# Rounding of the dense weights moved from ScalarE to transfers issued by GpSimd, and pooling of the first group's values by TensorE products

## The chip, the cores and the metric

One core of a Trainium2 chip runs the whole program. The metric is the device time of one execution in microseconds (us). The kernel before takes 1383.42 us, the median of three executions (1382.21 to 1384.28).

## The reference

Three layers on 4608 tokens (batch 8, sequence 576, 8 heads of 64, so d_model is 512):

```python
# attention with keys and values averaged over 8 neighbours in the sequence
k_p = k.reshape(B, H, Sp, 8, D).mean(axis=3)        # Sp = 72
v_p = v.reshape(B, H, Sp, 8, D).mean(axis=3)
attn = softmax(q @ k_p.T / sqrt(64)); x = attn @ v_p
# dense layer, 512 -> 2048 -> 512
h = x @ w_in
x = (maximum(h, 0) + log1p(exp(-abs(h)))) @ w_out
# eight experts, one for each token whose skip score is positive, 512 -> 1024 -> 512
out = x + gate * (maximum(x @ w1[e], 0) @ w2[e])
```

Inputs and outputs are float32. The program multiplies in the type fp32r after splitting each operand into a rounded part and the remainder (`wh` and `wl` for weights, `xh` and `xl` for tokens, `gh` and `gl` for the activation), with three products for each pair.

## The kernel before, in words

The tokens go through attention and the dense layer in nine groups of 512 (`for g in range(NG)`). For a group, `units_of` makes four units, one for each pair of heads: `unit0` for the first group, `unit` for the others. A unit is a Python generator; each `yield` hands over to the next piece of work, and `feed.tick()` advances all of them. The dense layer of a group has 16 chunks of 128 hidden columns. `p1(g, c)` makes twelve 128x512 products (L710), then softplus by three ScalarE activations (L713 to L715), a VectorE maximum-and-add (L716), the rounding of the result on ScalarE (L718) and its remainder on VectorE (L720). `p2(g, c)`, two chunks later, adds twelve products (L731 to L733) into four output banks. After the nine groups comes the expert layer.

The dense weights are loaded once, during the first group. They lie in memory as packed words, and `load_weights` unpacks them in steps that are interleaved with the first group's chunks: `unpack` is two ScalarE activations, `join` two VectorE operations. Chunks 0 to 3 take the path in halves of 512 columns (`half`). Chunks 4 to 15 are handled as six pairs `i` = 2 to 7: two 1 MB transfers (L506), then for each chunk of the pair `unpack` and `join` on 128x1024 into a scratch tile `v`; then for each chunk the rounded part by ScalarE (L519) and the remainder by VectorE (L520). The rounded and remainder parts land in the slot that held the packed words.

The values' pooling in `unit0`: `sums` adds groups of eight neighbours on VectorE (L553), `values` transposes the 72 sums with a TensorE transpose (L560) and copies the result out on ScalarE (L562). The attention weights are transposed by TensorE too (L607), after GpSimd has multiplied them (L546), and `output` makes the products L569.

Up to the expert layer a scheduler places the instructions: it sets the order of each engine's queue from the program and its own costs, so a line that moves in the program also moves lines around it. Each engine runs its queue strictly in order. Most plain transfers are issued by SP (SyncE); GpSimd's queue (POOL) holds the indirect transfers of the later stages and, in the first group, only the memset L643 and the multiplication L546 of each unit. The slots `w0` to `w7` of `wpool` hold one pair's weights each; during the first group's attention slots 5 to 7 serve as the room of `boot2`, `boot_kv` and `boot`.

Of the kernel before, what the change touches and what calls it, by code (L numbers as in the profile page):

```python
# [9 lines left out]
F32 = mybir.dt.float32  # L10
F32R = mybir.dt.float32r
BF16 = mybir.dt.bfloat16
I32 = mybir.dt.int32
U32 = mybir.dt.uint32
AF = mybir.ActivationFunctionType
# [5 lines left out]
P = 128  # L21
# [4 lines left out]
SP = 72  # L26
# [9 lines left out]
def tile_kernel(ctx, tc, qT, kT, vT, wbits, w9, w1, w2, out):  # L36
    nc = tc.nc
# [379 lines left out]
    def wtile(slot, name, *shape, dtype=F32):  # L417
        return wpool.tile([P, *shape], dtype, tag=f"w{slot}", name=name)

    with ExitStack() as ph:  # L420
# [29 lines left out]
        def room(tag, n, first):  # L450
            if first:
                taken[tag] += 1
                return boots[tag][(taken[tag] - 1) % len(boots[tag])][:, :n]
            pool = qp if tag in ("q", "st") else ep
            return pool.tile([P, n], F32, tag=tag, name=tag)
# [7 lines left out]
        def load_weights():  # L463


            bits = wbits.bitcast(I32)

            def unpack(lo, hi):
                nc.scalar.activation(out=hi.bitcast(F32), in_=hi.bitcast(F32), func=AF.Copy,
                                     scale=2.0 ** -112)  # L470
                nc.scalar.activation(out=lo, in_=lo.bitcast(U32), func=AF.Copy, scale=7.49 * 2.0 ** -32)

            def join(v, lo, hi):
                nc.vector.scalar_tensor_tensor(out=v, in0=hi, scalar=3, in1=lo,
                                               op0=ALU.logical_shift_left, op1=ALU.bitwise_or)
                nc.vector.scalar_tensor_tensor(out=v, in0=hi, scalar=-0x80000000, in1=v,
                                               op0=ALU.bitwise_and, op1=ALU.bitwise_or)

            def half(c, j, first):
                wh, wl = (wt[c // 2][:, c % 2, i, j * 512:(j + 1) * 512] for i in range(2))  # L480
                if first:
                    raw = room("raw", 1024, True).bitcast(I32).rearrange("p (a b) -> p a b", b=2)
                else:
                    raw = scratch.tile([P, 512, 2], I32, tag="raw", name="raw")
                nc.sync.dma_start(out=raw.rearrange("p a b -> p (a b)"),
                                  in_=bits[c * P:(c + 1) * P, j * 1024:(j + 1) * 1024])
                lo, hi = raw[:, :, 0], raw[:, :, 1]
                unpack(lo, hi)
                yield
                join(lo, lo, hi)  # L490
                nc.scalar.activation(out=wh, in_=lo.bitcast(F32), func=AF.Copy)
                yield
                nc.vector.tensor_tensor(out=wl, in0=lo.bitcast(F32), in1=wh.bitcast(F32),
                                        op=ALU.subtract)
                yield

            for i in range(EARLY // 2):
                wt.append(wtile(i, f"wt{i}", 2, 2, 1024, dtype=F32R))
            for c in range(EARLY):
                for j in range(2 if c >= LAG else 1):  # L500
                    yield from half(c, j, True)
            for i in range(EARLY // 2, 8):
                raw = wtile(i, f"raw{i}", 2, 1024, 2, dtype=I32)
                for j in range(2):
                    c = 2 * i + j
                    nc.sync.dma_start(out=raw[:, j].rearrange("p a b -> p (a b)"), in_=bits[c * P:(c + 1) * P, :])  # L506
                vs = []
                for j in range(2):
                    lo, hi = raw[:, j, :, 0], raw[:, j, :, 1]
                    unpack(lo, hi)  # L510
                    yield
                    v = scratch.tile([P, 1024], I32, tag="raw", name="v")
                    join(v, lo, hi)
                    vs.append(v.bitcast(F32))
                    yield
                wt.append(wtile(i, f"wt{i}", 2, 2, 1024, dtype=F32R))
                for j in range(2):
                    wh, wl = wt[i][:, j, 0], wt[i][:, j, 1]
                    nc.scalar.activation(out=wh, in_=vs[j], func=AF.Copy)  # L519
                    nc.vector.tensor_tensor(out=wl, in0=vs[j], in1=wh.bitcast(F32), op=ALU.subtract)  # L520
                    yield
            for c in range(LAG):
                yield from half(c, 1, False)
# [25 lines left out]
        def sums(us, vr):  # L549
            for u, *_ in us:  # L550
                kp, v, vp = pooled[u]
                if vp is None:
                    nc.vector.tensor_reduce(vr, v.rearrange("p (s w) -> p s w", w=8), AX.X, ALU.add)  # L553
# [21 lines left out]
        def unit0(hp, us, xh, xl):  # L575
# [20 lines left out]
            shares(e, sm, rc)  # L596
            yield
            yield
            vr = room("vr", SP, True)
            sums(us, vr)  # L600
            yield
            values(us, vr, ps_h, "h")
            et = room("et", 2 * G, True).rearrange("p (a k) -> p a k", a=2)[:SP]
            for h in range(2):
                tr = ps_a.tile([P, 512], F32, tag="pa", name="tr")
# [400 lines left out]
```

## Time and profile before

| | |
|---|---|
| median of three executions | 1383.42 us |
| the profiled execution, its own time | 1373.79 us |
| its span on the core | 1372.1 us |
| TensorE busy (PE) | 1333.0 us, 97% of the span |
| VectorE busy (DVE) | 850.9 us, 62% |
| ScalarE busy (ACT) | 595.4 us, 43% |
| GpSimd busy (POOL) | 312.6 us, 23% |
| mean granted TensorE clock | 0.992 |

The profile is one execution; its own time lies 9.6 us under the median, and its span 1.7 us under its own time. A share of busy time is a mean over very different stages: attention of the first group (0 to 37 us), the first group's dense layer with the loading of weights (37 to about 150 us), the other eight groups, and the experts. A row of the trace names an engine, a line, the operation and `out<-in`; PEld is TensorE's weight load, which runs beside PE.

### The profile page before, as it was taken

The numbers are of one execution on the slowest core, as the hardware profiler recorded it, in microseconds if no ns is written. First come the engines' busy times: TensorE is split into PE (matmuls) and PEld (weight loads), VectorE is DVE, ScalarE is ACT, GpSimd is POOL, SyncE is SP. The second block draws the span as 40 slices with busy tenths as digits, with TensorE's granted clock in tenths as the row PEclk, the third lists the DMA queues.
The fourth block names the chain that finished last, engine by engine and source line by source line (L and its number), as shares of the span: only waits on it lengthen the run. The fifth ranks groups of instructions, "written<-read, shape, count | busy, mean of one in ns | idle before, by whom it ended". The sixth has DMA issues, their size and how long they took to land. (4 is left out here: it accounts for less than half of the span.)

```text
span 1372.1 us, 21243 instructions
## 1 busy us (share of the span) xinstructions
PE 1333.0 (97%) x6970; PEld 1107.9 (81%) x6970; DVE 850.9 (62%) x1955; ACT 595.4 (43%) x1076; POOL 312.6 (23%) x374
## 2 busy tenths in 40 slices
PE   5989999999999999999999999999999999999986
PEld 3767877877877878878778778889999898989986
DVE  7997694784884974974955946555554432326254
ACT  6986544554544545455545445551111111114142
POOL 2000012021121121121030120243333343424343
PEclk9899999999999999999999999999999999999998
DMA  7643343142241241341430311503323222325272
GB/s 272 234 144 80 93 127 97 53 116 68 66 127 44 76 128 31 89 114 43 110 83 8 97 48 39 193 16 111 97 69 98 70 63 73 84 61 173 66 261 91
DMA packets 149599, 134.16 MB, mean 98 GB/s; under 512 B 100789, under 2 KB 116789, under 8 KB 146912
## 3 DMA queue, kind: packets, MB, share of 16 engines
q1 hardware_dynamic: 131744, 95.51, 24.1%
q0 software_dynamic: 17728, 37.13, 8.5%
q8 instruction: 59, 0.97, 0.3%
q14 instruction: 68, 0.56, 0.1%
HBM read 166.67 MB, written 29.67 MB: 143 GB/s over the span
## 5 line engine op out<-in xcount | busy, mean ns | idle before, releaser
L710 PE MATMUL h<-xh,wt 128*128 128x512 f32 x1152 | 381.6, 392 | 3.8 <-DVE a L716 3.8
L710 PEld LDWEIGHTS h<-xh,wt 128*128 128x128 f32 x1152 | 217.2, 189 | 52.3 <-DVE a L716 5.6
L731 PE MATMUL y<-wt,gh 128*128 128x512 f32 x576 | 232.7, 404 | 0.0
L889 PE MATMUL h<-xt,w1h 128*128 128x256 f32 x1280 | 227.9, 282 | 3.9 <-ACT w1h L404 2.1
L119 DVE CUSTOM_DVE_ANT_0 junk<-rows,w9b 128x512 bf16<-128x512 f32 x324 | 222.9, 688 | 8.1 <-ACT rows L113 3.2
L732 PE MATMUL y<-wt,gh 128*128 128x512 f32 x576 | 225.6, 392 | 0.0
L710 PE MATMUL h<-xl,wt 128*128 128x512 f32 x576 | 225.3, 391 | 0.0
L733 PE MATMUL y<-wt,gl 128*128 128x512 f32 x576 | 224.5, 390 | 0.3 <-DVE gl L720 0.3
L889 PEld LDWEIGHTS h<-xt,w1h 128*128 128x128 f32 x1280 | 197.5, 189 | 6.3 <-ACT w1h L404 2.5
L889 PE MATMUL h<-xt,w1l 128*128 128x256 f32 x640 | 180.3, 282 | 1.4 <-DVE w1l L405 0.8
L893 ACT ACTIVATE hs<-h 128x512 fp32r<-128x512 f32 x80 | 47.7, 598 | 298.7 <-PE h L889 222.3
L718 ACT ACTIVATE gh<-a 128x512 fp32r<-128x512 f32 x144 | 90.8, 631 | 167.8 <-DVE a L716 167.7
L716 DVE SCALAR_TENSOR_TENSOR a<-h,a 128x512 f32<-128x512 f32 x144 | 98.7, 685 | 100.2 <-ACT a L715 99.5
L713 ACT ACTIVATE a<-h 128x512 f32<-128x512 f32 x144 | 85.7, 595 | 172.2 <-PE h L710 171.6
L731 PEld LDWEIGHTS y<-wt,gh 128*128 128x128 f32 x576 | 108.1, 188 | 34.3 <-ACT a L713 7.4
L733 PEld LDWEIGHTS y<-wt,gl 128*128 128x128 f32 x576 | 108.1, 188 | 23.9 <-DVE gl L720 0.7
L710 PEld LDWEIGHTS h<-xl,wt 128*128 128x128 f32 x576 | 108.7, 189 | 22.8 <-issue 0.7
L732 PEld LDWEIGHTS y<-wt,gh 128*128 128x128 f32 x576 | 108.3, 188 | 20.7 <-issue 0.8
L889 PEld LDWEIGHTS h<-xt,w1l 128*128 128x128 f32 x640 | 122.8, 192 | 1.8 <-DVE w1l L405 1.0
L720 DVE TENSOR_TENSOR gl<-a,gh 128x512 fp32r<-128x512 f32 x144 | 99.3, 690 | 39.9 <-ACT gh L718 39.5
L917 DVE SCALAR_TENSOR_TENSOR ys<-y,xg 128x512 f32<-128x512 f32 x38 | 28.5, 751 | 147.3 <-PE y L915 147.3
L915 PE MATMUL y<-w2h,hs 128*128 128x512 f32 x304 | 118.4, 389 | 0.0
(196 smaller groups left out, 1817.3 us busy)
## 6 DMA issues: line engine op xcount, KB each, us to landing
w9b<-w SPq DMA_DIRECT2D x81, 256.0 KB
raw<-wbits SPq DMA_DIRECT2D x12, 1024.0 KB
x2d<-rows SPq DMA_DIRECT2D x36, 260.0 KB
et<-q SPq DMA_DIRECT2D x256, 32.0 KB
kv<-kT SPq DMA_DIRECT2D x28, 288.0 KB
kv<-vT SPq DMA_DIRECT2D x28, 288.0 KB
xm<-misc SPq DMA_DIRECT2D x160, 32.0 KB
misc<-misc SPq DMA_DIRECT2D x144, 32.0 KB
```

What stands on the lines that cost most here:

```text
L119: nc.vector.tensor_tensor_reduce(out=ws["junk"], in0=rows[t][:, :D], in1=w9b[e], scale=1.0, scalar=0.0, op0=ALU.mult, op1=ALU.add, accum_o ...
L710: nc.tensor.matmul(h, lhsT=l, rhs=r[:, kk, :], start=n == 0, stop=n == 11)
L713: nc.scalar.activation(out=a, in_=h, func=AF.Abs)
L716: nc.vector.scalar_tensor_tensor(out=a, in0=h, scalar=0.0, in1=a, op0=ALU.max, op1=ALU.add)
L718: nc.scalar.activation(out=gh, in_=a, func=AF.Copy)
L720: nc.vector.tensor_tensor(out=gl, in0=a, in1=gh.bitcast(F32), op=ALU.subtract)
L731: nc.tensor.matmul(y, lhsT=th, rhs=wh, start=c == 0, stop=False)
L732: nc.tensor.matmul(y, lhsT=th, rhs=wl, start=False, stop=False)
L733: nc.tensor.matmul(y, lhsT=tl, rhs=wh, start=False, stop=c == 15)
L889: nc.tensor.matmul(h[:, f2, :], lhsT=l, rhs=r[:, kk, :], start=n == 0, stop=n == 11)
L893: nc.scalar.activation(out=hh[:, fs, :], in_=h, func=AF.Relu)
L915: nc.tensor.matmul(y, lhsT=hl[:, f, js], rhs=ws["w2h"][:, f, :], start=False, stop=f == 7)
```

## The change

It has two parts.

First, the rounded part of the weights of chunks 4 to 15 is no longer made by ScalarE. After the second `join` of a pair, GpSimd issues two SBUF-to-SBUF transfers of 128x1024 float32 into fp32r, one for each chunk. The scratch tile `v` of pairs 3 to 5 comes from a new four-place tile `spare` in slot 7 (free by then); pairs 2, 6 and 7 still use the two-place scratch. The remainder on VectorE reads what the transfer wrote.

Second, in `unit0` the sum over eight neighbours and the transpose become eight accumulated products: the values, taken with a stride of eight, as the stationary operand (128x72) and the identity (128x128) as the moving one. They stand one `yield` earlier than the transpose did, and the copy to `vp` stands with them. The units of the other groups keep `sums` and `values`.

```diff
@@ load_weights @@
                 vs = []
+                if i == 3:
+                    spare = wtile(7, "spare", 4, 1024, dtype=I32)
                 for j in range(2):
                     lo, hi = raw[:, j, :, 0], raw[:, j, :, 1]
                     unpack(lo, hi)
                     yield
-                    v = scratch.tile([P, 1024], I32, tag="raw", name="v")
+                    if 3 <= i < 6:
+                        v = spare[:, 2 * (i % 2) + j]
+                    else:
+                        v = scratch.tile([P, 1024], I32, tag="raw", name="v")
                     join(v, lo, hi)
                     vs.append(v.bitcast(F32))
+                    if j == 1:
+                        wt.append(wtile(i, f"wt{i}", 2, 2, 1024, dtype=F32R))
+                        for k in range(2):
+                            nc.gpsimd.dma_start(out=wt[i][:, k, 0], in_=vs[k])
                     yield
-                wt.append(wtile(i, f"wt{i}", 2, 2, 1024, dtype=F32R))
                 for j in range(2):
                     wh, wl = wt[i][:, j, 0], wt[i][:, j, 1]
-                    nc.scalar.activation(out=wh, in_=vs[j], func=AF.Copy)
                     nc.vector.tensor_tensor(out=wl, in0=vs[j], in1=wh.bitcast(F32), op=ALU.subtract)
                     yield
@@ unit0 @@
             shares(e, sm, rc)
             yield
             yield
-            vr = room("vr", SP, True)
-            sums(us, vr)
-            yield
-            values(us, vr, ps_h, "h")
+            kp, v, _ = pooled[u]
+            v8 = v.rearrange("p (s w) -> p w s", w=8)
+            pv = ps_h.tile([P, 512], F32, tag="h", name="pv")
+            for w in range(8):
+                nc.tensor.matmul(pv[:SP, :P], lhsT=v8[:, w], rhs=ident, start=w == 0, stop=w == 7)
+            vp = pp.tile([SP, P], F32, tag="vp", name="vp")
+            nc.scalar.activation(out=vp, in_=pv[:SP, :P], func=AF.Copy)
+            pooled[u] = (kp, v, vp)
+            yield
             et = room("et", 2 * G, True).rearrange("p (a k) -> p a k", a=2)[:SP]
```

The scheduler then sets other orders up to the end of the first group's dense layer. Three places show it. In the rows of the changed kernel the line numbers are 7 to 12 higher: L523 is the new transfer, L527 the remainder (before L520), L553 the multiplication (L546), L655 the memset (L643), L610 the new product, L592 the scores (L585), L619 the transpose (L607), L576 the output (L569), L728 and L732 the two VectorE steps of softplus (L716 and L720), L651 and L652 the maximum and subtraction of a later unit (L639 and L640), L550 its sum (L543).

GpSimd's queue, after the four multiplications of the first group's units; before:

```order
L546 TENSOR_TENSOR boot_kv<-boot_kv,boot_171 128x576 x4
L643 MEMSET q 128x8x24
L546 TENSOR_TENSOR q<-q,st 128x8x72
L643 MEMSET q 128x8x24
L546 TENSOR_TENSOR q<-q,st 128x8x72
```

and in the changed kernel:

```order
L553 TENSOR_TENSOR boot_kv<-boot_kv,boot_171 128x576 x4
L655 MEMSET q 128x8x24
L523 DMA wt_485<-v 128x1024 x2
L553 TENSOR_TENSOR q<-q,st 128x8x72
L523 DMA wt_550<-spare 128x1024 x2
L523 DMA wt_620<-spare 128x1024 x2
L655 MEMSET q 128x8x24
L523 DMA wt_717<-spare 128x1024 x2
L553 TENSOR_TENSOR q<-q,st 128x8x72
L523 DMA wt_835<-v 128x1024 x2
```

The twelve issues stand in pairs between the multiplications of the second group's units, so a multiplication is now queued behind transfers that wait for a `join`.

VectorE's queue from the second `join` of pair 2 to its two remainders; before:

```order
L476 SCALAR_TENSOR_TENSOR v<-raw_426,v 128x1024
L720 TENSOR_TENSOR gl<-a,gh 128x512
L530 TENSOR_REDUCE kp<-kv 128x72
L520 TENSOR_TENSOR wt_487<-v,wt_487 128x1024
L716 SCALAR_TENSOR_TENSOR a<-h,a 128x512
L639 TENSOR_REDUCE st<-s 128x4 x2
L640 TENSOR_TENSOR q<-s,st 128x2x2x72
L720 TENSOR_TENSOR gl<-a,gh 128x512
L640 TENSOR_TENSOR q<-s,st 128x2x2x72
L520 TENSOR_TENSOR wt_487<-v,wt_487 128x1024
```

and in the changed kernel:

```order
L476 SCALAR_TENSOR_TENSOR v<-raw_450,v 128x1024
L651 TENSOR_REDUCE st<-s 128x4 x2
L732 TENSOR_TENSOR gl<-a,gh 128x512
L728 SCALAR_TENSOR_TENSOR a<-h,a 128x512
L652 TENSOR_TENSOR q<-s,st 128x2x2x72 x2
L474 SCALAR_TENSOR_TENSOR spare<-raw_516 128x1024
L732 TENSOR_TENSOR gl<-a,gh 128x512
L550 TENSOR_REDUCE st<-q 128x8
L527 TENSOR_TENSOR wt_485<-v,wt_485 128x1024
L551 TENSOR_SCALAR st<-st 128x8
L527 TENSOR_TENSOR wt_485<-v,wt_485 128x1024
```

Nine instructions of other work now stand between the `join` and the first remainder, where two stood; among them is the first `join` step of the next pair.

TensorE's queue in the first group's attention; before:

```order
L607 MATMUL tr<-ident,boot_kv 72x128 x8
L585 MATMUL s<-kbd_165,boot 128x144 x4
L585 MATMUL s<-kbd_167,boot 128x144 x2
L560 MATMUL pv<-ident,boot_171 72x128
L585 MATMUL s<-kbd_167,boot 128x144 x2
L607 MATMUL tr<-ident,boot_kv 72x128 x8
L560 MATMUL pv<-ident,boot_171 72x128
L569 MATMUL o<-boot,vp 64x512 x2
L607 MATMUL tr<-ident,boot_kv 72x128 x8
```

and in the changed kernel:

```order
L619 MATMUL tr<-ident,boot_kv 72x128 x6
L610 MATMUL pv<-ident,boot_kv 72x128 x8
L592 MATMUL s<-kbd_165,boot 128x144 x4
L619 MATMUL tr<-ident,boot_kv 72x128 x2
L610 MATMUL pv<-ident,boot_kv 72x128 x8
L592 MATMUL s<-kbd_167,boot 128x144 x4
L619 MATMUL tr<-ident,boot_kv 72x128 x8
L610 MATMUL pv<-ident,boot_kv 72x128 x8
L576 MATMUL o<-boot,vp 64x512 x2
L619 MATMUL tr<-ident,boot_kv 72x128 x8
L610 MATMUL pv<-ident,boot_171 72x128 x8
```

Two blocks of eight products now stand ahead of scores that stood behind transposes alone. After the first group's dense layer the queues hold the same instructions in the same order as before.

## Rows read from the trace of the kernel before

**Rows 1.** The page: TensorE's granted clock in 40 slices, in tenths.

```profile
PEclk9899999999999999999999999999999999999998
```

**Rows 2.** Busy time of each engine in five stretches of the first 200 us.

```profile
core 0: us, PE busy (x) PEld busy (x) DVE busy (x) ACT busy (x) POOL busy (x), PEclk, DMA share, GB/s
0.00:21.00 21.00, 10.30 (x41) 9.30 (x42) 13.79 (x31) 10.67 (x23) 5.78 (x43) 1.00 0.76 262
21.00:28.00 7.00, 3.46 (x23) 2.04 (x21) 6.42 (x15) 6.18 (x13) 1.71 (x1) 1.00 0.89 308
28.00:42.00 14.00, 13.28 (x38) 6.98 (x37) 12.10 (x20) 10.95 (x18) 1.15 (x1) 0.51 0.90 349
42.00:112.00 70.00, 62.34 (x279) 46.57 (x278) 65.39 (x85) 61.55 (x94) 5.58 (x6) 1.00 0.43 144
112.00:200.00 88.00, 87.98 (x409) 69.11 (x409) 69.35 (x154) 49.14 (x99) 6.98 (x9) 1.00 0.40 109
```

**Rows 3.** Waits of TensorE, 42 to 130 us: total, times, longest.

```profile
PE h L710 <- DVE a L716: 3.8, 3, 1.4
PE pv L560 <- DVE vr L553: 1.5, 3, 0.9
PE s L630 <- ACT kbd L538: 1.1, 2, 0.9
PE o L569 <- PE s L630: 1.0, 1, 1.0
```

**Rows 4.** Groups of instructions, 0 to 140 us: busy us and mean ns.

```profile
L585 PE MATMUL s<-kbd,boot 128*128 128x144 f32 x32 | 8.8, 455 | 5.4 <-ACT kbd L538 5.1 <-DVE boot L593 0.3
...
L519 ACT ACTIVATE wt<-v 128x1024 fp32r<-128x1024 f32 x12 | 12.1, 1053 | 0.3
...
L553 DVE TENSOR_REDUCE boot<-boot_kv 128x72 f32<-128x576 f32 x3 | 2.2, 745 | 0.0
...
L720 DVE TENSOR_TENSOR gl<-a,gh 128x512 fp32r<-128x512 f32 x15 | 10.3, 688 | 1.8 <-ACT gh L718 1.4
...
L639 DVE TENSOR_REDUCE st<-s 128x4 f32<-128x288 f32 x8 | 3.7, 458 | 1.6 <-PE s L630 1.4
...
L476 DVE SCALAR_TENSOR_TENSOR v<-raw,v 128x1024 int32<-128x1024 int32 x12 | 14.5, 1212 | 0.0
```

**Rows 5.** DMA from 20 to 130 us in 40 slices, and GpSimd's indirect issues: us to landing.

```profile
GB/s 109 281 433 334 161 408 417 417 313 12 23 260 316 375 340 57 30 44 45 423 131 173 420 277 3 0 39 39 33 172 136 8 0 106 31 42 34 236 257 47
...
xg<-x2d,ids POOLq DMA_INDIRECT x46, 4.1
...
out<-ys,ids POOLq DMA_INDIRECT x40, 2.9
...
ids<-tab,misc POOLq DMA_INDIRECT x24, 2.6
```

**Rows 6.** GpSimd's own time for an issue, min/median/max ns.

```profile
L348 POOL DMA_INDIRECT ids<-tab,misc x24: 992/998/1278, 864.3 to 1353.2; - x24
```

**Rows 7.** Timeline of TensorE in the first group's attention: start, length, instructions.

```profile
15.24 1.92 PE L607 MATMUL tr<-ident,boot_kv 128*72 128x128 f32 x8 [5.31 <-POOL boot_kv L546]
16.96 3.08 PE L585 MATMUL s<-kbd,boot 128*128 128x144 f32 x12
...
22.88 1.08 PE L569 MATMUL o<-boot,vp 72*64 72x512 f32 x4
26.95 1.07 PE L607 MATMUL tr<-ident,boot_kv 128*72 128x128 f32 x8 [3.00 <-POOL boot_kv L546]
...
28.92 1.97 PE L569 MATMUL o<-boot,vp 72*64 72x512 f32 x4 [0.72 <-ACT vp L562]
...
36.98 0.80 PE L710 MATMUL h<-xh,wt 128*128 128x512 f32 x1
```

**Rows 8.** Timeline of TensorE later in the first group.

```profile
41.73 0.63 PE L710 MATMUL h<-xh,wt 128*128 128x512 f32 x2
...
49.87 1.39 PE L630 MATMUL s<-kbd,q 128*64 128x144 f32 x8
...
58.62 0.39 PE L710 MATMUL h<-xh,wt 128*128 128x512 f32 x1
...
59.75 0.62 PE L710 MATMUL h<-xh,wt 128*128 128x512 f32 x2
```

## The prediction

> **What bounds the kernel now.** I began with the page's line of granted clock [rows 1]: full speed nearly everywhere, a dip in the second slice. TensorE is busy 97% of the span, so a gain must come from where it is not: the table by stretch [rows 2] has TensorE idle 10.7 of the first 21 us, 3.5 of the next 7, then a stretch of 14 us at a granted clock of 0.51 (the lower level, 1.2 GHz), then 7.7 idle of the 70 us in which the first group's dense layer runs beside the loading of weights. From 112 us on it is idle 0.02 of 88 us, so whatever the change saves or costs must arise before that, and stays to the end. In 42 to 112 us VectorE is busy 65.4 and ScalarE 61.6 of 70: both are nearly full. The waits [rows 3] name whom TensorE waits for there: 3.8 us for the softplus step L716, 1.5 for the sums of later units, 1.1 for a copy on ScalarE, 1.0 of its own. So this stage is bound by two full side engines, each a queue in strict order, and the stage before it by a chain through all engines.
>
> **The change, term by term.** The sum is made against the profiled execution (1373.8 us), and the difference is then put on the median, which lies 9.6 us higher.
>
> *ScalarE loses twelve activations.* They take 12.1 us in all [rows 4], nearly all between 42 and 112 us, where ScalarE goes from 61.6 to about 50 of 70. What comes back is at most TensorE's 7.7 us of idle time [rows 2], and at least nothing, if VectorE is the bound alone: the change takes no work from it there. VectorE has 4.6 us free in the stretch, and it can be no faster than without these. I take 4 us, near that ceiling, since the longest wait of TensorE is for a VectorE step that itself closes a chain of three ScalarE activations [rows 3]. Term: -4, bounds 0 and -7.7.
>
> *VectorE now waits for a transfer instead of an activation.* This wait is new, and VectorE's whole queue stands behind it. No transfer of this kind is in the trace. A small one issued by GpSimd lands after 2.6 us [rows 5], 1.0 of it GpSimd's own time [rows 6]; half a megabyte at 417 GB/s, the best slices while weights came in [rows 5], adds 1.3. So the first of a pair lands 3.9 us after its issue, the second 1.3 later, at 5.2. The cover stands in the order: for pair 2, nine VectorE instructions lie between the `join` and the first remainder. By rows of their size [rows 4] these are two of 0.46, two of 0.69, one like them, two more of about 0.46, one of 1.21 and one of 0.75, together 5.9 us. Other pairs have less, the shortest about 4.3 (three of 1.21 and one of 0.69). I reckon with 5 for the first and 6.2 for the second remainder, which follows one of 1.2. Then both transfers have landed, 1.0 early. Below: nothing is gained beyond the first term. Above: with the fixed part of the row gather (4.1 us for a quarter of a megabyte [rows 5], so 3.5 without its bytes) and half the rate, the second lands at 3.5 + 2 x 2.5 = 8.5, that is 2.3 late, six times: +14. I take 0, as the nearest row in kind is the store of a tile out of SBUF (2.9 us for a quarter of a megabyte [rows 5]), which gives the short end.
>
> *GpSimd's queue.* Twelve issues of 1.0 us [rows 6] enter an engine that is busy 5.6 of 70 us [rows 2]. A multiplication of the second group stands behind each pair or two of them, but the `join` for which they wait stands ahead of that multiplication's reciprocal in VectorE's queue, so it waits for little; at most two issues, 2 us, into a unit that has several chunks' time to spare. The traffic of 6.3 MB meets a DMA share of 0.43. SP's queue has the same transfers, a few in another order. Term 0; if this cover were gone, the second group's attention would be late by the 2 us, as the waits of TensorE for attention (L560, L630) already are by 1.5 and 1.1 [rows 3].
>
> *The first group's pooling.* VectorE loses four sums of 0.75, 3.0 us, while it is busy 6.4 of 7 us [rows 2, 4]. TensorE gets 32 products and loses four transposes. The scores L585 show 32 records [rows 4] for the 16 products of the order, so a float32 product is two records. A record of 144 columns took 3.08/12 = 0.257 us at 16.96 [rows 7], and 1.39/8 = 0.174 at 49.87 [rows 8]; for 128 columns and two records that is 0.46 or 0.31 a product, 3.7 or 2.5 us a unit. A transpose, 0.13 to 0.24 [rows 7], goes. The four units are 9 to 14 us of TensorE's time, three of them before 28 us, where 14 us are idle [rows 2]; one or two lie on the path. Bounds: -3.0 if all hide and VectorE's saving counts in full, +5 if two blocks of 2.5 are added. I take 0, the saving against one block.
>
> *The clock.* Ahead of the slow stretch TensorE ran eight transposes at 26.95 and had waited 3.0 us for GpSimd [rows 7]. Then four records of L569 took 1.97 us instead of the 1.08 before [rows 7]: with twelve such records in the stretch, 2.7 us lost. The products L710 took 4.75 us for eleven records (36.98 to 41.73 [rows 7, 8]) against 1.13 for five at full clock (58.62 to 59.75 [rows 8]), 2.3 us lost. Together 5.0. The changed queue puts a block of products where the engine idled and transposed. The bounds are 0 and -5.0; I take half, -2.5, as nothing shows how much is enough. The Trainium skill says on its page "TensorE: Matmul & The Clock Gate" (Part 4: PE-mode transpose) that transposes do not count as busy for the clock as products do; the trace agrees so far as the clock fell after a stretch that held transposes alone. By that rule the whole stretch might keep the higher level, and this term would be -5.0.
>
> Sum: -4 + 0 + 0 + 0 - 2.5 = -6.5. The profiled execution would go to 1367.3 us, the median to 1376.9, about **1377 us**.
>
> **The rivals.**
>
> *Late transfers* (0.22). Rounding on the way slows the transfer, or its landing is late while weights come in at over 400 GB/s. At the upper bound above VectorE stands 2.3 us at each of six pairs, +14, and the sum is +7.5: **1391 us**. It decides from 1.1 us of lateness a pair on, where 6 x 1.1 eats the gain. For it speaks that no such transfer is in the trace, and that the shortest cover is 4.3; against it the 2.9 us of the store.
>
> *VectorE is the bound alone* (0.10). It is busy 65.4 of 70 us, and ScalarE's relief gives nothing; the clock's 2.5 stays: **1381**. Against it: VectorE's rows show waits for ScalarE in their last column [rows 4].
>
> *The slow clock stays, and the products pay for it* (0.11). At 0.46 a product two blocks lie on the path, +5, the clock gives nothing, ScalarE's relief 4: **1384**. For it speaks the slow score records before 21 us [rows 7].
>
> *GpSimd is held while it writes descriptors* (0.05). If each issue waits for one VectorE instruction of 1.2 us, the second transfer of a pair lands 2.4 later, 1.4 past its cover, six times 8.4: **1385**. The rows speak against it: issues took 992 to 1278 ns, with a median at the low end, beside a busy VectorE [rows 6]. The Trainium skill has the rule on its page "SBUF — State Buffer" (the box on the "DVE blocks DMA" trap): a VectorE instruction in a mode that takes the shared port pair keeps GpSimd from writing descriptors. By this trace's issues the rule is not at work; no run so far shows it for direct transfers.
>
> **How the numbers follow.** The forecast has 0.52, the rivals the rest. A measurement of this kernel tells 0.2% from no change, 2.8 us. Faster by more: the forecast and half of the second rival, 0.57. Slower by more: late transfers, a third of the third rival and some of the fourth, 0.28. Within: 0.15. The range runs from 1371 (products hidden in part, the clock kept, 5.0 in the loaded stage, beyond which 1 in 10 is left) to 1393 (late transfers by a little more than the bound, 1 in 10 beyond). As cases of both signs hold most of the chance: the forecast's own range is 1371 to 1380.
>
> **What would show it.** Right: VectorE's remainders L527 start without waiting for a transfer, and the issues land within 5.2 us; the first L722 product starts near 35 us instead of 36.98; TensorE's idle time in the 70 us of the loaded stage halves; the slow stretch of the clock is shorter. Wrong: VectorE idle before L527 by more than 1 us a pair (late transfers); the loaded stage as long as before with VectorE at 70 of 70; first L722 later than 37 us with the granted clock low.

## The result, and the profile of the changed kernel

The changed kernel takes 1390.99 us, the median of six executions (1388.13 to 1396.3); the kernel before, on the same chip, 1383.89 (1382.21 to 1385.66). The ratio is 1.0057, with an interval of 1.0044 to 1.007: slower by about 8 us. The forecast was 1377, so its sign was wrong; the time is that of the rival with late transfers (1391).

Its profiled execution took 1391.68 us, 17.9 more than the one of before. Only half of that belongs to the change. The row of TensorE's products into `h` gives the first and the last start of them; the last is the end of the dense layer, behind which both programs are the same. The kernel before:

```profile
L710 PE MATMUL h<-xh,wt x1152: 387/389/796, 37.0 to 910.1; 128*128 128x512 f32 x192
```

and the changed one:

```profile
L722 PE MATMUL h<-xh,wt x1152: 387/389/796, 37.2 to 919.0; 128*128 128x512 f32 x192
```

8.9 us are lost there, close to the medians' 7.1 and the ratio's 7.9. The rest arises in the experts, and most of it goes with the chip, not with the program: behind this mark the profiled executions of e1 to e7, all on one chip, took 462.4 to 464.6 us, those of e8, e8b and e10 on another 470.0 to 475.5, and the kernel before has a median of 1373.8 to 1374.4 us on the first and 1382.7 on the second. So below each run is given by its ratio and by this mark (the **dense end**, 910.1 before). The mark is that of one execution and moves by itself: in e4, which runs the changed kernel's program up to there, the first dense product starts at 35.8 us instead of 37.2. A difference of 1 to 2 us in it tells little.

The page's clock line, then the table by stretch, against [rows 1, 2]:

```profile
PEclk9989999999999999999999999999999999999999
```

```profile
0.00:21.00 21.00, 9.80 (x41) 8.99 (x42) 12.74 (x28) 9.20 (x20) 5.78 (x43) 1.00 0.75 262
21.00:28.00 7.00, 7.00 (x55) 6.99 (x55) 6.01 (x14) 6.20 (x14) 1.15 (x1) 1.00 0.88 297
28.00:42.00 14.00, 13.68 (x76) 9.31 (x75) 11.75 (x20) 13.19 (x23) 1.43 (x1) 1.00 0.86 318
42.00:112.00 70.00, 57.13 (x229) 42.92 (x227) 54.25 (x70) 44.19 (x73) 9.02 (x15) 0.85 0.66 224
112.00:200.00 88.00, 87.82 (x407) 68.11 (x407) 68.79 (x141) 50.41 (x98) 7.78 (x11) 1.00 0.38 105
```

Up to 42 us the change does good: TensorE is full in 21 to 28 us and the granted clock stays at 1.00 where it was 0.51. Then 42 to 112 us turns bad: TensorE idle 12.9 us instead of 7.7, its clock 0.85 instead of 1.00, and VectorE at 54 and ScalarE at 44 of 70: no engine is full any more. The waits say why: VectorE's (42 to 112 us)

```profile
DVE wt L527 <- DMA wt<-v: 6.6, 2, 5.5
DVE wt L527 <- DMA wt<-spare: 3.0, 2, 2.7
```

and TensorE's (42 to 130 us), against [rows 3]:

```profile
PE s L642 <- ACT kbd L545: 7.1, 3, 5.2
PE h L722 <- DVE a L728: 4.9, 2, 4.2
```

VectorE's timeline shows the two places, pair 2 at 56 us and pair 4 at 83:

```profile
44.14 1.22 DVE L476 SCALAR_TENSOR_TENSOR v<-raw,v 128x1024 int32<-128x1024 int32 x1
...
50.05 0.75 DVE L550 TENSOR_REDUCE st<-q 128x8 f32<-128x576 f32 x1
56.34 1.22 DVE L527 TENSOR_TENSOR wt<-v,wt 128x1024 fp32r<-128x1024 f32 x1 [5.54 <-DMA wt<-v]
57.49 0.16 DVE L551 TENSOR_SCALAR st<-st 128x8 f32<-128x8 f32 x1
58.75 1.22 DVE L527 TENSOR_TENSOR wt<-v,wt 128x1024 fp32r<-128x1024 f32 x1 [1.10 <-DMA wt<-v]
...
83.24 1.23 DVE L527 TENSOR_TENSOR wt<-spare,wt 128x1024 fp32r<-128x1024 f32 x1 [2.70 <-DMA wt<-spare]
84.38 0.75 DVE L537 TENSOR_REDUCE kp<-kv 128x72 f32<-128x576 f32 x1
```

and TensorE's what follows from each:

```profile
60.70 0.79 PE L722 MATMUL h<-xh,wt 128*128 128x512 f32 x1 [4.24 <-DVE a L728]
...
61.72 1.05 PE L722 MATMUL h<-xh,wt 128*128 128x512 f32 x2
...
69.33 0.61 PE L722 MATMUL h<-xh,wt 128*128 128x512 f32 x2
...
85.75 2.48 PE L642 MATMUL s<-kbd,q 128*64 128x144 f32 x8 [5.17 <-ACT kbd L545]
```

A softplus step stood behind pair 2's remainder, so TensorE idled 4.24 us and then ran at the lower level (two products in 1.05 us, later 0.61). At pair 4 it was a key sum of the second group's attention, L537; TensorE idled 5.17 us and again ran at the lower level (eight score records in 2.48 us, against 1.39 in [rows 8]).

Why pair 2 was late is seen on the queues. GpSimd's issue of pair 2 in the changed kernel's timeline, then SP's of weight loads:

```profile
46.27 1.34 POOL L523 DMA_DIRECT2D wt<-v  x2 [0.41 <-DVE st L651]
```

```profile
33.34 2.16 SPq L506 DMA_DIRECT2D raw<-wbits  x4
...
41.50 1.28 SPq L506 DMA_DIRECT2D raw<-wbits  x3
```

In the kernel before, SP issues the three loads of pairs 5 and 6 after the place where pair 2 is rounded:

```profile
50.28 1.28 SPq L506 DMA_DIRECT2D raw<-wbits  x3
```

In the changed kernel they go 8.8 us earlier, ahead of pair 2's transfers. The DMA queues (packets, MB, share of the 16 engines; q1 is SP's, q0 GpSimd's), first for 46.3 to 50.3 us, then for 50.3 to 59:

```profile
q1 hardware_dynamic: 316, 1.54, 101.9%
```

```profile
q1 hardware_dynamic: 252, 1.76, 51.8%
q0 software_dynamic: 288, 1.05, 32.4%
```

For 4 us after its issue not one packet of the rounding transfer ran: the weight loads had all 16 engines. Then the two shared them. VectorE went on at 56.34, 10.1 us after the issue.

At pair 4, issued at 76.44 us, the first packet came 4.2 us after the issue too, but there the engines had room for part of that time (78.4 to 80.4 us):

```profile
q1 hardware_dynamic: 170, 0.44, 72.8%
```

So that the engines are full is not all of it; what holds the first packet stays open. That it goes with SP's loads shows in all traces: in ten cases behind such loads, in six kernels, it came 4.0 to 4.9 us after the issue; elsewhere 1.1 to 1.3, but for 1.8 in e2 (pair 4) and 2.6 in e13 (pair 3).

### The profile page after: what moved, and what is told of

Read it like the earlier page. It is cut to its first block, busy times and chain, and to the rows that moved or that the text cites. A ratio compares the mean times of both kernels' runs of the same rounds, so it can differ in the third digit from the quotient of the medians.

```text
span 1390.0 us, 21390 instructions
## 1 busy us (share of the span) xinstructions
PE 1343.1 (97%) x7030; PEld 1116.4 (80%) x7030; DVE 846.2 (61%) x1951; ACT 583.8 (42%) x1064; POOL 314.9 (23%) x386
## 5 line engine op out<-in xcount | busy, mean ns | idle before, releaser
L728 DVE SCALAR_TENSOR_TENSOR a<-h,a 128x512 f32<-128x512 f32 x144 | 98.5, 684 | 105.0 <-ACT a L727 101.4
L732 DVE TENSOR_TENSOR gl<-a,gh 128x512 fp32r<-128x512 f32 x144 | 99.1, 688 | 40.1 <-ACT gh L730 36.8
L926 PE MATMUL y<-w2l,hs 128*128 128x512 f32 x304 | 118.4, 390 | 0.3 <-issue 0.3
```

The lines of the kernel that those rows point to most:

```text
L728: nc.vector.scalar_tensor_tensor(out=a, in0=h, scalar=0.0, in1=a, op0=ALU.max, op1=ALU.add)
L732: nc.vector.tensor_tensor(out=gl, in0=a, in1=gh.bitcast(F32), op=ALU.subtract)
L926: nc.tensor.matmul(y, lhsT=hh[:, f, js], rhs=ws["w2l"][:, f, :], start=False, stop=False)
```

## The experiments

The theory: two of the six pairs (2 and 4) are issued while weight loads fill the DMA engines, so they land late; VectorE's queue stands, TensorE starves, its clock falls. Rivals: a rounding transfer is slow in itself; the pooling products cost; GpSimd is held. Each ratio is against the kernel before on the same chip (its medians there: 1373.8 to 1386.5 us).

| run | ratio, interval | dense end (before 910.1) |
|---|---|---|
| e1 pooling alone | 0.9969 [0.9958, 0.9981] | 907.3 |
| e2 transfers alone | 1.0044 [1.0031, 1.0057] | 915.7 |
| e3 pairs 2 and 4 by ScalarE | 0.9974 [0.9965, 0.9984] | 906.5 |
| e4 plain copies | 1.0068 [1.0053, 1.0083] | 917.9 |
| e5 loads held by VectorE | 1.0052 [1.0039, 1.0065] | 918.7 |
| e6 VectorE doesn't wait | 0.9975 [0.9965, 0.9986] | 905.6 |
| e7 pair 2 alone | 1.0008 [0.9999, 1.0018] | 911.3 |
| e8 one remainder on GpSimd | 1.0005 [0.9996, 1.0015] | 911.1 |
| e8b both remainders on GpSimd | 1.0032 [1.0021, 1.0044] | 916.9 |
| e9 one product | (not comparable) | 908.9 |
| e10 ScalarE's rounding twice | 1.0028 [1.0016, 1.004] | 912.8 |
| e11 pair 2 alone, pair 5's loads held | 1.0015 [1.0006, 1.0024] | 912.5 |
| e12 pair 2 alone, loads behind it | 0.9944 [0.993, 0.9957] | 905.3 |
| e13 all pairs, loads behind them | 0.9999 [0.9987, 1.001] | 906.7 |

**e1, pooling alone.** The kernel before with the second part of the change, whose core is

```diff
-            vr = room("vr", SP, True)
-            sums(us, vr)
...
+            for w in range(8):
+                nc.tensor.matmul(pv[:SP, :P], lhsT=v8[:, w], rhs=ident, start=w == 0, stop=w == 7)
```

> The kernel before with the pooling part alone (eight products with the identity in the first group's four units; the weights still rounded by ScalarE). Late transfers (my theory of the loss: the two late pairs of transfers, 2 and 4, cost everything): the profile after shows the granted clock at 1.00 in 28 to 42 us instead of 0.51 and chunks 1 to 3 about 2 us early, and nothing else of this part later; so about 2 us less than before (ratio 0.998 to 0.999), chunk 4 and all later ones 2 us early. Products cost: the 32 products are what moved the scheduler's order and cost the time, then slower than before by several us (ratio 1.003 to 1.006).

Faster by 4.2 us (1370.21 against 1374.44), more than the 2 expected. The clock stays up, and the loaded stage is as before:

```profile
28.00:42.00 14.00, 13.68 (x75) 9.33 (x75) 11.73 (x20) 13.17 (x23) 1.43 (x1) 1.00 0.86 304
42.00:112.00 70.00, 62.63 (x281) 46.62 (x280) 66.41 (x86) 61.41 (x96) 5.10 (x6) 1.00 0.44 155
```

The products don't cost.

**e2, transfers alone.** The kernel before with the first part:

```diff
+                        for k in range(2):
+                            nc.gpsimd.dma_start(out=wt[i][:, k, 0], in_=vs[k])
...
-                    nc.scalar.activation(out=wh, in_=vs[j], func=AF.Copy)
```

> The kernel before with the transfers alone (the first group's pooling as before, by VectorE sums and a transpose). Late transfers: the slow clock of 28 to 42 us is as before, pairs 2 and 4 land 7 to 12 us after their issue, VectorE stands before the remainders for some 8 us in all, and the time is 8 to 12 us over the kernel before (ratio 1.006 to 1.009), so more than with both parts. Products cost: about as before or faster (ratio 0.997 to 1.000), as ScalarE is relieved of 12 us and nothing was added to TensorE.

Slower by 6.0 us, less than expected, and by another pair. SP's three loads go out at 49.85 us here, behind pair 2's issue (47.26), and pair 2 is on time; pair 4 costs 3.8:

```profile
52.54 1.22 DVE L527 TENSOR_TENSOR wt<-v,wt 128x1024 fp32r<-128x1024 f32 x1
...
79.55 1.23 DVE L527 TENSOR_TENSOR wt<-spare,wt 128x1024 fp32r<-128x1024 f32 x1 [3.76 <-DMA wt<-spare]
```

So it is the pooling part that moves the three loads forward (e1 has them at 41.31 too), and the loss at pair 2 needs both parts.

**e3, pairs 2 and 4 by ScalarE.**

```diff
-                        for k in range(2):
-                            nc.gpsimd.dma_start(out=wt[i][:, k, 0], in_=vs[k])
+                        if i not in (2, 4):
+                            for k in range(2):
+                                nc.gpsimd.dma_start(out=wt[i][:, k, 0], in_=vs[k])
...
+                    if i in (2, 4):
+                        nc.scalar.activation(out=wh, in_=vs[j], func=AF.Copy)
```

> The changed kernel, but pairs 2 and 4 are rounded by ScalarE again; pairs 3, 5, 6 and 7 by transfers. Late transfers, because pairs 2 and 4 alone meet a full queue of weight loads: VectorE waits for transfers under 1 us in all in 42 to 112 us, no new stretch of slow clock, and the time is 4 to 6 us below the kernel before (ratio 0.9955 to 0.997): the clock's 2, and eight activations fewer on ScalarE. Rounding slow in itself (every transfer of this kind is late when VectorE has little else to do): the other four pairs then make VectorE stand 1 to 3 us each, and the time stays 3 us or more above the kernel before (ratio over 1.002). Products cost: also above the kernel before.

Faster by 3.6 us, just short of the 4 to 6 expected, with 0.9 us of waits for transfers: the other four pairs do no harm that the time shows. But it is no better than e1, though ScalarE has eight activations fewer, and against the expectation a stretch of slow clock came (a mean of 0.95 in 42 to 112 us).

**e4, plain copies.**

```diff
-                            nc.gpsimd.dma_start(out=wt[i][:, k, 0], in_=vs[k])
+                            nc.gpsimd.dma_start(out=wt[i][:, k, 0].bitcast(F32), in_=vs[k])
```

> The changed kernel with the same twelve transfers in the same order, but as plain float32 copies without rounding (left out: the rounding; the rounded parts hold unrounded words and the remainders are zero). Rounding slow in itself: the transfers land earlier and the time falls by several us, towards the kernel before (ratio 1.002 or less). Late behind the weight loads: a copy of the same bytes is as late, pairs 2 and 4 again land 7 to 12 us after their issue, VectorE stands before the remainders for some 8 to 11 us, and the time is that of the changed kernel (ratio 1.0045 to 1.007).

As slow as the changed kernel; VectorE waits 5.08 and 1.22 us at pair 2 and 2.7 at pair 4. Rounding on the way is not what makes them late.

**e5, loads held by VectorE.**

```diff
                 raw = wtile(i, f"raw{i}", 2, 1024, 2, dtype=I32)
+                if i in (5, 6):
+                    o = 2 if i == 5 else 4
+                    for j in range(2):
+                        nc.vector.tensor_copy(raw[:, j, 0:1, 0], wt[o][:, 1, 1, 0:1].bitcast(I32))
```

> The changed kernel with all six pairs rounded by transfers, but the packed weight loads of pair 5 are held until pair 2's remainders are done, and those of pair 6 until pair 4's (a one-column VectorE copy into the place that the load will fill makes the load wait; eight such copies of about 0.1 us are added). Late transfers behind the weight loads: pair 2 now lands within 3 to 5 us of its issue instead of 10.0 and 11.7, pair 4 within 3 to 5 instead of 6.8 and 7.5, VectorE's standing before the remainders falls from 11 us to under 3, and the time falls to 2 to 6 us below the kernel before (ratio 0.9955 to 0.9985), unless the loads of pairs 5 and 6 themselves then come late. Rounding slow in itself: the landing of pairs 2 and 4 stays over 6 us and the time stays at that of the changed kernel (ratio about 1.005).

The edit makes four copies, not eight. The time did not fall, but for a reason that the trace shows: pair 2 is on time (no wait; chunk 4 at 55.5 us, before at 58.6), while the held loads, issued at 67.5 and 87.3 us, now run ahead of pairs 4 and 5 (issued at 68.73 and 89.07), and these wait:

```profile
77.29 1.23 DVE L531 TENSOR_TENSOR wt<-spare,wt 128x1024 fp32r<-128x1024 f32 x1 [5.84 <-DMA wt<-spare]
...
99.14 1.23 DVE L531 TENSOR_TENSOR wt<-spare,wt 128x1024 fp32r<-128x1024 f32 x1 [6.37 <-DMA wt<-spare]
```

The lateness goes with the loads, not with the pair.

**e6, VectorE doesn't wait.**

```diff
-  nc.vector.tensor_tensor(out=wl, in0=vs[j], in1=wh.bitcast(F32), op=ALU.subtract)
+  nc.vector.tensor_tensor(out=wl, in0=vs[j], in1=vs[j], op=ALU.subtract)
```

> The changed kernel, but the remainder subtracts the unrounded value from itself and so reads nothing that a transfer writes (left out: the true remainders; they are zero). The twelve transfers still run, and late ones still delay the products that read them. VectorE's queue standing behind the transfer is what costs: the loss goes, no wait of VectorE for a transfer, TensorE idle under 8 us in 42 to 112 us, and the time is 4 to 8 us below the kernel before (ratio 0.994 to 0.997), since now pooling's 4 us, which the kernel with pooling alone showed, and ScalarE's relief both count. Late weights at the products themselves, or the transfers' traffic, are what costs: the time stays over the kernel before (ratio over 1.002). If it comes out at the 0.997 of pooling alone, ScalarE's relief is worth nothing.

The loss is gone, though the transfers run and pair 2's land as late (issued at 45.37 us, their packets run from 49.5 to about 56.5): it is VectorE's queue behind the transfer that costs. It comes out at e1's 0.997, and TensorE's idle time is e1's too (7.5 and 7.4 us of 70), with ScalarE at 51 instead of 61:

```profile
42.00:112.00 70.00, 62.50 (x282) 47.65 (x283) 64.44 (x84) 51.16 (x84) 11.27 (x16) 1.00 0.66 222
```

ScalarE's relief is worth 1.7 us by the dense end, which is within what that mark moves by itself, and nothing that the ratios tell apart.

**e7, pair 2 alone by transfers.**

```diff
+                        if i == 2:
+                            for k in range(2):
+                                nc.gpsimd.dma_start(out=wt[i][:, k, 0], in_=vs[k])
...
+                    if i > 2:
+                        nc.scalar.activation(out=wh, in_=vs[j], func=AF.Copy)
```

> The changed kernel with transfers for pair 2 alone; pairs 3 to 7 are rounded by ScalarE. Late behind the weight loads: pair 2 lands 8 to 12 us after its issue as seven weight loads are under way, VectorE stands some 5 to 7 us before its two remainders, chunk 4 starts some 4 us later than in the kernel with pooling alone, a stretch of slow clock may follow, and the time is 3 to 6 us over pooling alone (ratio 0.9990 to 1.0015 against the kernel before). Nothing that belongs to one late pair (a cost spread over all twelve transfers): within 1.5 us of pooling alone (ratio 0.996 to 0.998).

VectorE waits 5.66 and 0.95 us, and the time is 1.0008: 5.3 us over e1 by the ratios, 4.0 by the dense end. One late pair costs that.

**e8 and e8b, remainders on GpSimd**, to see whether VectorE bounds the stage (e1, with the second chunk's subtraction, then both, on GpSimd).

```diff
-                    nc.vector.tensor_tensor(out=wl, in0=vs[j], in1=wh.bitcast(F32), op=ALU.subtract)
+                    eng = nc.gpsimd if j == 1 else nc.vector
+                    eng.tensor_tensor(out=wl, in0=vs[j], in1=wh.bitcast(F32), op=ALU.subtract)
```

> Pooling alone (no transfers), and the remainder of the second chunk of each pair is made by GpSimd instead of VectorE, so VectorE loses six subtractions of 1.22 us, 7.3 us of its 66.4 in 42 to 112 us, where GpSimd is busy 5.1. VectorE alone bounds the stage with the weights (the reason why relieving ScalarE gave nothing): TensorE's 7.4 us of idle time there falls by 2 to 5, and the time comes 2 to 5 us under that of pooling alone (ratio 0.993 to 0.9955 against the kernel before). A chain through both engines, where no single engine's work counts: within 1.5 us of pooling alone (ratio 0.996 to 0.998). GpSimd's subtraction, an estimated 2.5 us by the 1.4 of a multiplication of 576 columns, slowing VectorE or coming late: above pooling alone.

> As the run before it, with the remainders of both chunks of each pair on GpSimd: VectorE loses 14.6 us, GpSimd gets an estimated 30 us more in some 90 us. VectorE alone bounds: 3 to 7 us under pooling alone (ratio 0.992 to 0.995), with VectorE at about 52 to 55 of 70 us and TensorE idle under 4. A chain through both engines: within 1.5 us of pooling alone. GpSimd late: its queue also holds the second group's multiplications, so products wait for a remainder and the time comes above pooling alone.

Both are slower than e1, by 5.0 and 8.7 us by the ratios. They don't answer the question, as VectorE was held up in a new way. In e8b, GpSimd's two subtractions end at 65.85 us:

```profile
61.12 4.73 POOL L520 TENSOR_TENSOR wt<-v,wt 128x1024 fp32r<-128x1024 f32 x2 [5.92 <-ACT wt L519]
...
63.57 3.37 DVE L474 SCALAR_TENSOR_TENSOR v<-raw 128x1024 int32<-128x1024 int32 x1 [3.25 <-POOL wt L520]
```

VectorE first waits 3.25 us for the scratch that the first subtraction reads, and then an instruction whose median is 1.22 us takes 3.37: it ends 1.1 us after GpSimd's second subtraction.

**e9, one product instead of eight** (on e1).

```diff
-            for w in range(8):
-                nc.tensor.matmul(pv[:SP, :P], lhsT=v8[:, w], rhs=ident, start=w == 0, stop=w == 7)
+            for w in range(1):
+                nc.tensor.matmul(pv[:SP, :P], lhsT=v8[:, w], rhs=ident, start=True, stop=True)
```

> Pooling alone (no transfers), with one product with the identity in each unit instead of eight (left out: seven eighths of each pooled sum of the first group). TensorE loses 28 products before 37 us; VectorE is relieved as with eight. The clock is what pooling gains, because the products fill TensorE's queue: with one product the granted clock falls to 0.5 for a stretch between 21 and 42 us as in the kernel before, and the time comes back to 1 to 3 us over pooling alone (ratio 0.998 to 0.9995). VectorE's relief is what it gains (four sums of 0.75 us less in a chain that was nearly full): the time stays within 1 us of pooling alone, or below (ratio 0.9955 to 0.9975), whatever the clock does.

The whole time can't be compared: with other values other tokens reach the experts, 84 blocks instead of 80. By the dense end it is 1.6 us worse than e1, and the clock is down again:

```profile
28.00:42.00 14.00, 13.72 (x37) 7.42 (x38) 10.45 (x16) 9.99 (x16) 1.43 (x1) 0.63 0.95 369
```

The first dense product starts at 35.22 us, sooner than e1's 37.0, and still more than half of e1's gain by this mark (1.6 of 2.8 us) is gone. That the clock carries most of what pooling by products brings is likely by this, but rests on one execution of each kernel.

**e10, ScalarE's rounding twice** (on e1).

```diff
                     nc.scalar.activation(out=wh, in_=vs[j], func=AF.Copy)
+                    nc.scalar.activation(out=wh, in_=vs[j], func=AF.Copy)
```

> Pooling alone (no transfers), with each of ScalarE's twelve roundings of 1.01 us made twice: ScalarE gets 12 us more, some 61 to 70 of 70 us in the stage with the weights. ScalarE has slack there (relieving it gave nothing): within 1.5 us of pooling alone, at most 2 (ratio 0.996 to 0.9985). ScalarE is as much a bound as VectorE, and the transfers' relief was lost in other ways: 4 us or more above pooling alone (ratio 0.9995 or over), since the engine was already busy 61.4 of 70 us.

It is over e1 by 8.1 us by the ratios, 5.5 by the dense end, with VectorE waiting 5.5 us for the rounding. ScalarE has no slack to give away, though relieving it gave little. The second rounding also lengthens the chain ahead of each remainder; how much is the load and how much the chain isn't told apart.

**e11, pair 2 alone, pair 5's loads held** (on e7).

```diff
+                if i == 5:
+                    for j in range(2):
+                        nc.vector.tensor_copy(raw[:, j, 0:1, 0], wt[2][:, 1, 1, 0:1].bitcast(I32))
```

> The kernel with transfers for pair 2 alone (which cost 5.3 us over pooling alone: 1374.5 against 1370.2), with one thing more: the packed weight loads of pair 5 wait for pair 2's remainders, so that they are no longer under way when pair 2's transfers are issued. Late behind the weight loads: pair 2 lands in under 5 us instead of 12.0, VectorE does not wait for it, no slow clock follows, and the time returns to that of pooling alone (ratio 0.996 to 0.9985), if pair 5's loads, now later, still come in time. Any cause in the transfers themselves, or in VectorE's wait of any length: the time stays at 1.0 to 1.002.

(The 5.3 us named there is that of the ratios; the two medians differ by 4.3.) It did not take the cause away: pair 6's loads moved up in SP's queue (issued at 36.41 and 37.03 us), and VectorE again waited 4.90 us.

**e12, pair 2 alone, the loads behind it.** On e7; SP's order is kept, and the loads of pairs 5 and 6 wait until pair 2's transfers have landed.

```diff
                 raw = wtile(i, f"raw{i}", 2, 1024, 2, dtype=I32)
+                if i in (5, 6):
+                    for j in range(2):
+                        nc.gpsimd.tensor_copy(raw[:, j, 0:1, 0], wt[2][:, 1, 0, 0:1].bitcast(I32))
```

> Transfers for pair 2 alone, with the weight loads of pairs 5 and 6 held until pair 2's transfers have landed (four one-column copies on GpSimd, which read what the transfer wrote; SP's queue keeps its order). Late behind the weight loads: under 1 MB of weight loads is left when pair 2 is issued, it lands in under 5.5 us, VectorE waits under 1 us for it, chunk 4 starts 2 to 4 us before that of the kernel before, and the time is that of pooling alone (ratio 0.9955 to 0.9985). The transfer itself, or the traffic of any kind: landing over 8 us, ratio 1.000 to 1.002 as without the hold.

The loads go at 52.13 us. The transfers, issued at 45.08, have their first packet 1.3 us later instead of 4.1 (e7) and nearly no other traffic (45.1 to 51.2 us), and VectorE, with the same instructions between, doesn't wait:

```profile
q0 software_dynamic: 288, 1.05, 48.7%
q1 hardware_dynamic: 197, 0.28, 12.3%
```

```profile
48.87 0.74 DVE L556 TENSOR_REDUCE st<-q 128x8 f32<-128x576 f32 x1
49.62 1.22 DVE L533 TENSOR_TENSOR wt<-v,wt 128x1024 fp32r<-128x1024 f32 x1
50.77 0.17 DVE L557 TENSOR_SCALAR st<-st 128x8 f32<-128x8 f32 x1
50.84 1.22 DVE L533 TENSOR_TENSOR wt<-v,wt 128x1024 fp32r<-128x1024 f32 x1
```

The same transfers, 0.9944 instead of 1.0008: better than expected, faster than both kernels and all other versions, and 6.0 us by the dense end better than e7. It also answers the rival of a held GpSimd: beside the same work of VectorE, GpSimd's transfers now start and land in time.

**e13, all pairs by transfers, the loads behind them** (as e12; pair 6's second load behind pair 4).

```diff
+                        o = wt[4 if i + j == 7 else 2]
+                        nc.gpsimd.tensor_copy(raw[:, j, 0:1, 0], o[:, 1, 0, 0:1].bitcast(I32))
```

> The changed kernel with all six pairs by transfers, the weight loads of pair 5 and the first of pair 6 held until pair 2 has landed, the second of pair 6 until pair 4 has. Late behind the weight loads: pairs 2 and 4 land within 5.5 us, VectorE's waits for transfers in 42 to 112 us fall from 9.6 to under 3 us, and the time is at or a little under that of pooling alone, as in the run where nobody waited for a transfer (ratio 0.995 to 0.9985). The transfers themselves: ratio 1.004 to 1.007 as in the changed kernel. If a held load now comes late for its own unpacking, or meets another pair, that pair's wait shows it, and the time lies between.

Pairs 2 and 4 are on time (waits of 0.44 and 0); pair 3, now behind the held loads, waits 1.94 and 0.76. The waits for transfers in 42 to 112 us are 3.4 us in all, against 9.6. The dense end is 906.7, 12.3 us better than the changed kernel's and level with e1 and e3. The ratio is 0.9999, no better than the kernel before and worse than both the expectation and this mark; where the 3 us go behind the dense layer stays open.

## Why the prediction was wrong, point by point

*VectorE waits for a transfer: the step that failed.* The prediction had the transfers land 3.9 and 5.2 us after their issue, within a cover of 5 and 6.2. The cover was nearly right: pair 2's other work ran to 50.80 us, 5.4 us from the end of the `join` at 45.36, and 4.5 from the issue at 46.27, which came 0.9 after that end. The landing was right at pairs 3, 5 and 6: both transfers were in place 4.0 to 4.7 us after the issue, and VectorE never stood over 0.3 us (pair 7, after 112 us, cost it 1.5). At pairs 2 and 4 VectorE could go on only 10.1 and 6.8 us after the issue. What was left out of this term, put at 0, is the wait behind loads already under way; the price came from a row without them.

*GpSimd's queue, "SP's queue has the same transfers, a few in another order".* This sentence, priced at 0, holds the cause: the few were three weight loads of 1 MB that passed from behind pair 2's rounding to ahead of it. The DMA share of 0.43 quoted beside it is a mean over 70 us; in 46.3 to 50.3 it was 1.0. That GpSimd itself costs shows nowhere, as forecast (VectorE waits 0.8 us for its multiplications up to 150 us, before 1.3); an issue takes it 0.53 to 0.77 us instead of the 1.0 assumed:

```profile
L523 POOL DMA_DIRECT2D wt<-v x6: 530/578/767, 46.3 to 126.9; - x6
```

*The rival.* Its 1391 us was met by luck, for its picture was not met: two pairs were late, by 6.6 and 2.7 us, not six by 2.3. Of its two conditions only the late landing held (e4 rules out slow rounding). And a wait did not cost its own length. Pair 2 alone cost 4 to 5.3 us for 6.6 of waiting (e7 over e1); the other five pairs cost 6.8 to 7.7 more, where only 3.0 of waiting are added in 42 to 112 us. The price arises in TensorE: it idled 5.2 us more in the stage, and a mean clock of 0.85 is 21 of 70 us at the lower level (70 x 0.15 / 0.5).

*ScalarE's relief, -4.* Over-sized. e6, without waits, gives 0 (ratio) to 1.7 us (dense end) over e1. TensorE's wait for the softplus step was read as a wait for ScalarE, since ScalarE's activations stand in that chain; but in e6 ScalarE itself idles 9.4 us for products. That VectorE is the bound alone (the second rival) isn't shown: e8 and e8b couldn't tell, and e10 says that ScalarE counts as well. And e12, which relieves ScalarE of two activations only, is 2.0 (dense end) to 3.4 us (ratio) better than e1, more than e6 with all twelve; what it gains by, other than the loads held back, stays open.

*Pooling, 0.* Right. The records' own lengths of 0.30 to 0.34 us overlap; the first block of 16 takes 3.62 us (at 17.03), the others 2.33 (below), so a product 0.45 or 0.29, about the 0.46 or 0.31 reckoned. The four blocks keep TensorE busy 10.6 us, inside the 9 to 14:

```profile
L610 PE MATMUL pv<-ident,boot_kv 128*72 128x128 f32 x48 | 8.3, 339 | 0.0
...
L610 PE MATMUL pv<-ident,boot 128*72 128x128 f32 x16 | 2.3, 298 | 0.0
```

Three blocks lie before 28.5 us, where TensorE idled before; the fourth, at 30.40, lies in the stretch that the clock now shortens.

*The clock, -2.5.* Right in kind, and nearly in size. The whole stretch keeps 1.00, and e1, which has this term and the pooling alone, gives 2.8 us by the dense end, 4.2 by the ratio; the bound of -5.0 wasn't reached. The four records of L569 that took 1.97 us [rows 7] take 1.08 now:

```profile
26.23 2.33 PE L610 MATMUL pv<-ident,boot_kv 128*72 128x128 f32 x16
28.49 1.08 PE L576 MATMUL o<-boot,vp 72*64 72x512 f32 x4
...
37.17 0.50 PE L722 MATMUL h<-xh,wt 128*128 128x512 f32 x1 [0.32 <-DVE xl L579]
```

The first dense product is not earlier (37.17 against 36.98), though only 0.32 us of that is a wait for VectorE; the 35 us that should have shown the prediction right did not come in this execution (e4 has 35.8).

## What to carry to other kernels

When work moves from an engine to a transfer, ask what is in the DMA engines at the microsecond of its issue, not what their mean share is: a pair of transfers that takes 4.0 to 4.7 us from its issue where no loads are ahead (pairs 3, 5 and 6) took 12 behind 3.3 MB of them (1.54 + 1.76, pair 2). Read the order of every queue that feeds the same engines, also for transfers that the diff doesn't touch, and hold the loads that nobody needs yet: with pair 2 alone on transfers, that turned 1.0008 into 0.9944 with four one-column copies. With all six pairs it only brought the time back to that of the kernel before (e13). And where two side engines work in strict order, relieving one of them can give far less than the work taken off it: here 12 us less work for at most 1.7 us.

## What the runs showed of the hardware

A rounding transfer from SBUF to SBUF is hardly slower than a plain one: its packets of 4 KB took 176 ns, a plain one's 159 (medians, the changed kernel and e4), and the kernels' times aren't told apart (1.0057 and 1.0068). Behind SP's loads, GpSimd's transfers of pair 2 got no packet for 4 us and then about 4 parts in 10 of the bytes (1.05 of 2.83 MB). The Trainium skill says on its page "DMA: Bandwidth & Descriptors" (Queues, rings and completion order) that each DMA engine takes turns between its queues, a packet at a time. The trace agrees from 50.3 us on, so far as both queues run side by side (36 and 34 packets of the trace in 53 to 54 us). The 4 us before are not in that rule; whether GpSimd's queue had anything to hand over by then, the trace does not show.

A VectorE instruction that began during a GpSimd subtraction lasted until 1.1 us after its end, nearly its own full length (e8b). The Trainium skill's page "SBUF — State Buffer" (SBUF: two separate sides, the list that reads its diagram) calls the port pair that the two share an exclusive lock, held for a whole instruction, also where VectorE's instruction has two inputs in SBUF and GpSimd's reads SBUF, as both do here; the row agrees.
